# Transposes from the matrix engine to DMA, Q projection spread over the attention tiles, W_down in half blocks

## The chip, the cores and the metric

The kernel runs on one core of a Trainium2 chip. The metric is device time in microseconds (us). A run is one timed execution; medians over several runs are quoted, and verdicts use runs of the normal (fast) state. PE is the matrix engine (TensorE), DVE is VectorE, ACT is ScalarE, POOL is GpSimd, SP is SyncE, which issues the DMAs here.

## The reference

One transformer block with linear attention, S = 2048 tokens, D = 1024, 32 heads of 32, F = 3584, all in bf16:

```python
def _A_ref(x, wqkv, wo):                    # attention
    q, k, v = split_heads(x @ wqkv)         # shortened
    phi = lambda t: jnp.where(t > 0, t + 1, jnp.exp(t)) + 1e-6
    pq, pk = phi(q), phi(k)
    kv = jnp.einsum("bhsd,bhse->bhde", pk, v)
    z = jnp.einsum("bhsd->bhd", pk)
    num = jnp.einsum("bhqd,bhde->bhqe", pq, kv)
    den = jnp.einsum("bhqd,bhd->bhq", pq, z)[..., None] + 1e-6
    return merge_heads(num / den) @ wo      # shortened

h  = x + _A_ref(_layernorm(x), A_wqkv, A_wo)
n  = _layernorm(h)
gate = n @ W_gate; gate = gate * (gate > 0)
h2 = h + (gate * (n @ W_up)) @ W_down
```

(The last three lines are condensed from the reference's second function.)

## The kernel before

It has five stages: a start in which weights and the first rows of x arrive; K and V projections for 16 tiles of 128 tokens, accumulating `kv`; the Q projection of four blocks of 512 tokens together with attention (`nd` computes numerator and denominator and divides, `wo_h` projects and adds x); gate and up products in a Strassen-like form with seven products per block; and the down product in the same form. The matrix products here contract over the partitions (the first axis of a tile), so three tensors must be turned: normalised x (`xn` to `xnT`), the attention output (`o_sb` to `oT`) and normalised h (`hn`). Before, PE turns all of them in 128x128 blocks, 384 in all, and ScalarE (in the first tile VectorE too) copies the result out of PSUM, the memory that PE writes to.

```python
            xn = awork.tile([P, D], BF16, tag="xn", name="xn")
            nc.vector.tensor_scalar(out=xn[:], in0=x_sb[:], scalar1=mv[:, 0:1], scalar2=rstd[:],
                                    op0=ALU.subtract, op1=ALU.mult)
            pt = ps_tp()
            for kc in range(KC):
                nc.tensor.transpose(pt[:, kc, :], xn[:, kc * P:(kc + 1) * P], ident[:])
                if t == 0 and KC >= 2 and kc == KC // 2 - 1:
                    nc.vector.tensor_copy(out=xnT[:, 0:KC // 2, t * P:(t + 1) * P], in_=pt[:, 0:KC // 2, :])
            if t == 0 and KC >= 2:
                nc.scalar.copy(out=xnT[:, KC // 2:KC, t * P:(t + 1) * P], in_=pt[:, KC // 2:KC, :])
            else:
                nc.scalar.copy(out=xnT[:, :, t * P:(t + 1) * P], in_=pt[:])
    # ... cut ...
        ln_T(0)
        for g in range(NTB):
            pks = {}
            for tt in range(TPB):
                t = g * TPB + tt
                if t + 1 < ST:
                    ln_T(t + 1)
                pks[t] = kproj(t)
            for tt in range(TPB):
                t = g * TPB + tt
                vproj_kv(t, pks.pop(t))
            if g < NQA - 1:
                q_proj(g, ps_mm)
        for c in range(KC):
            bnk, i = divmod(c, GPB)
            nc.vector.tensor_tensor(out=kvz[:, c, :], in0=kv_ps[bnk][:, i * NDW:(i + 1) * NDW],
                                    in1=mask[:], op=ALU.mult)
        q_proj(NQA - 1, ps_mm)

    q_proj_rest = range(NQA, NTB)
    for b in q_proj_rest:
        q_proj(b, ps_y)
    qctx.close()
    # ... cut ...
        def nd():
            # ...
            for cs in nd_groups:
                ng = len(cs)
                ps = ps_x("nd")
                for k, c in enumerate(cs):
                    nc.tensor.matmul(ps[:, k * NDW:(k + 1) * NDW], lhsT=pqT[:, c, t * P:(t + 1) * P],
                                     rhs=kvz[:, c, :], start=True, stop=True)
                ndv = ps[:, 0:ng * NDW].rearrange("p (g w) -> p g w", w=NDW)
                den_sb = bsmall.tile([P, GPB, HPC], FP32, tag="den_sb", name="den_sb")
                nc.vector.tensor_scalar_add(out=den_sb[:, :ng, :], in0=ndv[:, :, P:NDW], scalar1=DEN_EPS)
                rd = bsmall.tile([P, GPB, HPC], FP32, tag="rd", name="rd")
                nc.vector.reciprocal(out=rd[:, :ng, :], in_=den_sb[:, :ng, :])
                nc.vector.tensor_tensor(
                    out=o_sb[:, cs[0] * P:(cs[-1] + 1) * P].rearrange("p (g h e) -> p g h e", g=ng, h=HPC),
                    in0=ndv[:, :, 0:P].rearrange("p g (h e) -> p g h e", h=HPC),
                    in1=rd[:, :ng, :].unsqueeze(3).to_broadcast([P, ng, HPC, Dh]),
                    op=ALU.mult)
    # ... cut ...
        def oT():
            pt = ps_tp()
            for c in range(KC):
                nc.tensor.transpose(pt[:, c, :], st["o"][:, c * P:(c + 1) * P], ident[:])
            st["oT"] = bwork.tile([P, KC, P], BF16, tag="oT", name="oT")
            nc.scalar.copy(out=st["oT"][:], in_=pt[:])

        def wo_h():
            x_sb = bwork.tile([P, D], BF16, tag="x_res", name="x_res")
            nc.sync.dma_start(out=x_sb[:], in_=xf[t * P:(t + 1) * P, :])
            h_sb = bwork.tile([P, D], BF16, tag="h", name="h")
            nwo = D // NW
            stats = bsmall.tile([P, nwo, nc.vector.BN_STATS_DIM], FP32, tag="stats2", name="stats2")
            for j in range(nwo):
                ps = ps_y("attn")
                for c in range(KC):
                    nc.tensor.matmul(ps[:, :NW], lhsT=st["oT"][:, c, :], rhs=wo_sb[:, c, j * NW:(j + 1) * NW],
                                     start=(c == 0), stop=(c == KC - 1))
    # ... cut ...
        def hnT():
            pt2 = ps_tp()
            for kc in range(KC):
                nc.tensor.transpose(pt2[:, kc, :], st["hn"][:, kc * P:(kc + 1) * P], ident[:])
            for j in range(2):
                nc.scalar.copy(out=hnq[s][i][j][:, :, r:r + P], in_=pt2[:, j * KH:(j + 1) * KH, :])
    # ... cut ...
    LAG = (0, 1, 1, 3)
    for step in range(ST + max(LAG)):
        for k in range(4):
            n = step - LAG[k]
            if 0 <= n < ST:
                stages[n][k]()
                if k == 3 and (n + 1) % (ST // NS) == 0:
                    hn_sums(n // (ST // NS))
    # ... cut ...
        def snap(ps, nm):
            m = mwork.tile([P, 2, SW], FP32, tag=nm, name=nm)
            nc.scalar.copy(out=m[:], in_=ps[:])
            return m
    # ... cut ...
        for k, h in ((0, 0), (1, 0), (0, 1), (1, 1)):
            x = dpool.tile([P, FH, DW], BF16, tag="wd", bufs=5, name="wd")
            nc.sync.dma_start(out=x[:], in_=wd_v[:, k * FH:(k + 1) * FH, h * DW:(h + 1) * DW])
            b.append(x)
        b11, b21, b12, b22 = b
```

The lag table runs the four stages of attention tiles in a software pipeline: in a step, tile n's `nd` is followed by `oT` and `wo_h` of tile n−1 and `hnT` of tile n−3. `_xy`, `ps_x`, `ps_y` and `ps_tp` give out PSUM banks.

Of the kernel before, what the change touches and what calls it, by code (L numbers as in the profile page):

```python
# [8 lines left out]
ALU = mybir.AluOpType  # L9
# [22 lines left out]
def block_kernel(ctx: ExitStack, tc: tile.TileContext, x, wqkv, wo, wg, wu, wd, out, H: int):  # L32
# [7 lines left out]
    assert Dh == 32 and D % P == 0 and S % P == 0 and F % P == 0  # L40
# [4 lines left out]
    TB = min(512, S)  # L45
    NTB = S // TB
    TPB = TB // P
    HB = min(256, TB)
    NHB = TB // HB
    NW = min(512, D)  # L50
    NKB = D // NW
    CPB = NW // P
    NDW = P + HPC
    GPB = 512 // NDW
    n_kv_banks = (KC + GPB - 1) // GPB
    assert TPB * H <= 512

# [9 lines left out]
    for hh in range(HPC):  # L67
        nc.gpsimd.memset(mask[hh * Dh:(hh + 1) * Dh, hh * Dh:(hh + 1) * Dh], 1.0)
        nc.gpsimd.memset(mask[hh * Dh:(hh + 1) * Dh, P + hh:P + hh + 1], 1.0)

    psctx = ExitStack()
    pspool = psctx.enter_context(tc.tile_pool(name="ps", bufs=1, space=PSUM))
    _xy = [0]

    def ps_tp():
        return pspool.tile([P, KC, P], BF16, tag="tp", bufs=2, name="tp")

    def ps_x(nm="x"):
        return pspool.tile([P, 512], FP32, tag="x", bufs=2, name=nm)

    def ps_y(nm="y"):
        return pspool.tile([P, 512], FP32, tag="y", bufs=4, name=nm)

    def ps_xy(nm="xy"):
        _xy[0] += 1
        return ps_x(nm) if _xy[0] % 3 != 0 else ps_y(nm)
# [5 lines left out]
    wo_sb = pq_pool.tile([P, KC, D], BF16, name="wo_sb")  # L92

    def phi_from_psum(ps_ap, dst_ap, pool, width):
        e = pool.tile([P, width], FP32, tag="phi_e", name="phi_e")
        nc.scalar.activation(out=e[:], in_=ps_ap, func=ACT.Exp)  # L96
        e2 = pool.tile([P, width], FP32, tag="phi_e2", name="phi_e2")
# [5 lines left out]
    qctx = ExitStack()  # L103
    qpool = qctx.enter_context(tc.tile_pool(name="qpool", bufs=1))
    qwork = qctx.enter_context(tc.tile_pool(name="qwork", bufs=2))
    wq_sb = qpool.tile([P, KC, D], BF16, name="wq_sb")
    xnT = qpool.tile([P, KC, S], BF16, name="xnT")
    wqkv_v = wqkv.rearrange("(kc p) n -> p kc n", p=P)

    def q_proj(b, ps_fn):  # L110
        for c in range(KC):
            ps = ps_fn("qp")
            for kc in range(KC):
                nc.tensor.matmul(ps[:, :TB], lhsT=wq_sb[:, kc, c * P:(c + 1) * P],  # L114
                                 rhs=xnT[:, kc, b * TB:(b + 1) * TB],
                                 start=(kc == 0), stop=(kc == KC - 1))
            phi_from_psum(ps[:, :TB], pqT[:, c, b * TB:(b + 1) * TB], qwork, TB)

    NQA = min(2, NTB)

    with ExitStack() as actx:
        apool = actx.enter_context(tc.tile_pool(name="apool", bufs=1))
        xpool = actx.enter_context(tc.tile_pool(name="xpool", bufs=min(6, ST)))
        awork = actx.enter_context(tc.tile_pool(name="awork", bufs=2))
        asmall = actx.enter_context(tc.tile_pool(name="asmall", bufs=4))

        ps_mm = ps_xy
        wkv_sb = apool.tile([P, KC, 2 * D], BF16, name="wkv_sb")
        kv_ps = [ps_y("kv_ps") for _ in range(n_kv_banks)]

# [6 lines left out]

        load_x(0)
        nxt = 1
        for j in range(NKB):  # L140
            nc.sync.dma_start(out=wkv_sb[:, :, j * NW:(j + 1) * NW],
                              in_=wqkv_v[:, :, D + j * NW:D + (j + 1) * NW])
            if nxt < min(TPB, ST):
                load_x(nxt)
                nxt += 1
        while nxt < min(TPB, ST):
            load_x(nxt)
            nxt += 1
        for j in range(NKB, 2 * NKB):
            nc.sync.dma_start(out=wkv_sb[:, :, j * NW:(j + 1) * NW],  # L150
                              in_=wqkv_v[:, :, D + j * NW:D + (j + 1) * NW])
        while nxt < min(6, ST):
            load_x(nxt)
            nxt += 1
        for j in range(NKB):
            nc.sync.dma_start(out=wq_sb[:, :, j * NW:(j + 1) * NW], in_=wqkv_v[:, :, j * NW:(j + 1) * NW])
        nc.sync.dma_start(out=wo_sb[:], in_=wo.rearrange("(kc p) n -> p kc n", p=P))

        def ln_T(t):
# [3 lines left out]
            nsub = (D + 511) // 512  # L163
            fm = D // nsub
            stats = asmall.tile([P, nsub, nc.vector.BN_STATS_DIM], FP32, tag="stats", name="stats")
            for i in range(nsub):
                nc.vector.bn_stats(out=stats[:, i, :], in_=x_sb[:, i * fm:(i + 1) * fm])  # L167
            mv = asmall.tile([P, nc.vector.BN_AGGR_DIM], FP32, tag="mv", name="mv")
            nc.vector.bn_aggr(out=mv[:], in_=stats[:])
            lnv = asmall.tile([P, 1], FP32, tag="lnv", name="lnv")  # L170
            nc.scalar.activation(out=lnv[:], in_=mv[:, 1:2], func=ACT.Ln, bias=LN_EPS, scale=1.0)
            rstd = asmall.tile([P, 1], FP32, tag="rstd", name="rstd")
            nc.scalar.activation(out=rstd[:], in_=lnv[:], func=ACT.Exp, scale=-0.5)
            xn = awork.tile([P, D], BF16, tag="xn", name="xn")
            nc.vector.tensor_scalar(out=xn[:], in0=x_sb[:], scalar1=mv[:, 0:1], scalar2=rstd[:],  # L175
                                    op0=ALU.subtract, op1=ALU.mult)
            pt = ps_tp()
            for kc in range(KC):
                nc.tensor.transpose(pt[:, kc, :], xn[:, kc * P:(kc + 1) * P], ident[:])  # L179
# [442 lines left out]
```

## Time and profile before

| | before |
|---|---|
| median of the first three runs | 828.26 us (827.77 to 830.4) |
| profiled run, span | 825.0 us |
| PE busy | 782.2 us (95%) |
| largest single PE wait | 8.0 us, for the first block of W_down |

The page's head and its line for the engines: busy time, share of the span, and number of instructions of each engine.

```profile
span 825.0 us, 10025 instructions
...
PE 782.2 (95%) x4016; PEld 369.1 (45%) x4016; DVE 506.7 (61%) x845; ACT 216.2 (26%) x337; POOL 3.6 (0%) x31
```

PE works 95% of the time, so there are 43 us of gaps to win, and beyond them only work taken off PE. The next view lists what PE waited for: the waiting group, the releaser, total us, how many waits, the longest.

```profile
engine line waited for: us in total, times, longest us
PE attn L315 <- ACT oT L304: 10.7, 15, 1.1
PE accA L510 <- DMA wd<-in_B_W_down_dram: 8.0, 1, 8.0
PE tp L179 <- DVE xn L175: 6.3, 2, 6.1
PE nd L286 <- DVE o_sb L293: 4.8, 5, 1.3
PE tp L335 <- DVE hn L328: 2.4, 1, 2.4
```

In attention PE waits for ScalarE's copies of the turned attention output (10.7 us in 15 waits) and for the division on VectorE (4.8). At the first down product it waits 8.0 us once, for a DMA of W_down.

Where PE is not the limit shows in windows cut at the stages: start, K/V, the two Q blocks after it, attention, gate/up, down. Each line gives the window, its length, each engine's busy us with the number of instructions, the granted PE clock (1.00 is full), the mean busy share of the DMA engines, and GB/s.

```profile
core 0: us, PE busy (x) PEld busy (x) DVE busy (x) ACT busy (x) POOL busy (x), PEclk, DMA share, GB/s
0.00:10.60 10.60, 1.98 (x16) 1.55 (x17) 4.37 (x9) 2.68 (x6) 1.58 (x17) 1.00 0.89 294
10.60:153.80 143.20, 143.00 (x820) 70.67 (x818) 68.85 (x139) 61.48 (x115) 2.00 (x14) 1.00 0.20 67
153.80:196.50 42.70, 41.38 (x194) 18.68 (x193) 30.96 (x68) 13.73 (x23) 0.00 (x0) 1.00 0.44 118
196.50:298.60 102.10, 82.88 (x641) 47.18 (x640) 91.17 (x248) 36.59 (x81) 0.00 (x0) 0.98 0.22 76
298.60:649.50 350.90, 341.72 (x1569) 154.07 (x1569) 218.50 (x300) 101.72 (x112) 0.00 (x0) 0.99 0.19 58
649.50:825.00 175.50, 171.25 (x784) 76.93 (x784) 92.79 (x85) 0.00 (x0) 0.00 (x0) 0.99 0.49 162
```

In K/V PE is busy 143.0 of 143.2 us: there, work removed from PE is time removed. In attention (196.5 to 298.6) PE is busy 82.88 of 102.1 us and VectorE 91.17. Just before it, in the Q blocks, PE is full (41.38 of 42.7) and VectorE is not.

The groups of PE's transposes (line, engine, operation, names, shapes, count, then busy us, mean ns, idle time before):

```profile
line engine op names shapes xcount | busy us, mean ns | idle before us <-releasers
...
L179 PE MATMUL tp<-ident,xn 128*128 128x128 bf16 x128 | 11.1, 230 | 8.6 <-DVE xn L175 6.3 <-DVE xnT L181 2.3
L302 PE MATMUL tp<-ident,o_sb 128*128 128x128 bf16 x128 | 10.7, 218 | 0.0
L335 PE MATMUL tp<-ident,hn 128*128 128x128 bf16 x128 | 9.9, 219 | 2.4 <-DVE hn L328 2.4
```

They cost 31.7 us of PE, or 83 ns each (11.1 / 128 = 87, 9.9 / 128 = 77); the mean of one record, about 220 ns, includes pipelined overlap and must not be multiplied by the count. Last, two DMA issues, for scale (size, and median us from issue to landing):

```profile
DMA packets 75678, 74.04 MB, mean 90 GB/s; under 512 B 3440, under 2 KB 67952, under 8 KB 75120
...
x_res<-in_A_x_dram SPq DMA_DIRECT2D x16, 256.0 KB, 2.8
...
h_dram_1891<-h SPq DMA_DIRECT2D x1, 256.0 KB, 2.0
```

### The profile page before, as it was taken

The page shows a single profiled execution, that of the slowest core. Times are in us where ns is not written, and L with a number is a line of the kernel's source. Part 1 is how long each engine was busy: PE and PEld are TensorE (multiplying, and loading weights), DVE is VectorE, ACT ScalarE, POOL GpSimd, SP SyncE. Part 2 cuts the span into 40 slices and gives each one's busy share as a digit, 9 for nine tenths or more (in the row PEclk, how much of TensorE's full clock was granted, in tenths as well). Part 3 has the DMA queues.
Part 4 walks back from the last instruction along what each step waited for, and adds up shares of the span by engine and source line. Part 5 has one row for each costly group of instructions (what it writes and reads, how often), then busy time and mean ns, then how long its engine had stood idle before and what let it go on. Part 6 is the DMA issues. An engine that isn't in the chain of part 4 may idle for free.

```text
span 825.0 us, 10025 instructions
## 1 busy us (share of the span) xinstructions
PE 782.2 (95%) x4016; PEld 369.1 (45%) x4016; DVE 506.7 (61%) x845; ACT 216.2 (26%) x337; POOL 3.6 (0%) x31
## 2 busy tenths in 40 slices
PE   5999999998897979999999999999999699999998
PEld 3445554443454534444444444444444244444443
DVE  5756314386999965567657556765754784329832
ACT  3435434332334333322323332333332000000000
POOL 0000000000000000000000000000000000000000
PEclk9999999999999989999999999999999899999999
DMA  9700000530222200040401304040000983892001
GB/s 323 250 14 26 1 1 1 152 92 0 97 83 79 89 25 14 20 127 27 122 26 56 84 20 128 25 122 27 20 19 20 300 267 120 273 340 97 26 33 45
DMA packets 75678, 74.04 MB, mean 90 GB/s; under 512 B 3440, under 2 KB 67952, under 8 KB 75120
## 3 DMA queue, kind: packets, MB, share of 16 engines
q1 hardware_dynamic: 75632, 73.41, 27.9%
q8 instruction: 31, 0.51, 0.3%
q14 instruction: 15, 0.12, 0.1%
HBM read 57.67 MB, written 15.73 MB: 89 GB/s over the span
## 4 chain that ended last, share of the span: by engine, by line
PE 59%; DVE 2%; DMA 2%; issue 1%; ACT 0%; SPq 0%; ACTq 0%
PE A L396 24%; PE E L396 12%; PE accA L510 10%; PE Dp L396 6%; PE accE L510 6%; PE accD L510 1%; DMA wd<-in_B_W_down_dram 1%; DMA hres<-h_dram_1898 1%; DVE s_6330 L534 0%; DVE hh L536 0%; DVE o L522 0%; DVE wd L548 0%; DVE s_6331 L535 0%; ACT u_5732 L410 0%; DVE hh_5749 L447 0%
## 5 line engine op out<-in xcount | busy, mean ns | idle before, releaser
L510 PEld LDWEIGHTS <-hh 128*128 128x128 bf16 (+1 forms) x560 | 55.1, 99 | 75.5 <-issue 10.6
L510 PE MATMUL accA<-wd,hh 128*128 128x512 f16 (+1 forms) x336 | 74.9, 385 | 8.0 <-DMA wd<-in_B_W_down_dram 8.0
L315 PE MATMUL attn<-wo_sb,oT 128*128 128x512 bf16 x256 | 61.2, 387 | 10.8 <-ACT oT L304 10.7
L396 PEld LDWEIGHTS <-tg 128*128 128x128 f16 x448 | 43.8, 98 | 54.2 <-issue 1.4
L396 PEld LDWEIGHTS <-tu 128*128 128x128 f16 x448 | 43.8, 98 | 52.9
L205 PE MATMUL vp<-wkv_sb,xnT 128*128 128x512 bf16 x256 | 59.8, 379 | 0.0
L192 PE MATMUL kp<-wkv_sb,xnT 128*128 128x512 bf16 x256 | 59.6, 388 | 0.0
L114 PE MATMUL qp<-xnT,wq_sb 128*128 128x512 bf16 x256 | 56.2, 379 | 1.3 <-DVE pqT L100 1.3
L396 PEld LDWEIGHTS <-wg 128*128 128x128 bf16 x336 | 33.2, 99 | 41.6 <-issue 2.9
L396 PEld LDWEIGHTS <-wu 128*128 128x128 bf16 x336 | 33.2, 99 | 40.9 <-issue 2.2
L315 PEld LDWEIGHTS <-oT 128*128 128x128 bf16 x256 | 23.6, 99 | 38.2 <-ACT oT L304 13.6
L114 PEld LDWEIGHTS <-wq_sb 128*128 128x128 bf16 x256 | 24.9, 98 | 30.9 <-issue 1.9
L192 PEld LDWEIGHTS <-xnT 128*128 128x128 bf16 x256 | 25.0, 100 | 28.0 <-issue 2.2
L205 PEld LDWEIGHTS <-xnT 128*128 128x128 bf16 x256 | 24.0, 97 | 24.6
L445 ACT ACTIVATE rg<-A 128x512 bf16<-128x512 f32 x28 | 16.7, 597 | 68.1 <-PE A L396 68.1
L304 ACT COPY oT<-tp 128x1024 bf16<-128x1024 bf16 x16 | 16.2, 1012 | 55.9 <-PE tp L302 55.9
L417 DVE SCALAR_TENSOR_TENSOR hh<-gu 128x512 bf16<-128x512 bf16 x42 | 29.0, 690 | 1.0
L96 ACT ACTIVATE phi_e<-qp 128x512 f32<-128x512 f32 x32 | 19.1, 597 | 39.1 <-PE qp L114 37.8
L175 DVE TENSOR_SCALAR xn<-x_sb,mv,rstd 128x1024 bf16<-128x1024 bf16 x16 | 8.7, 544 | 33.4 <-PE tp L179 31.1
L208 ACT CAST v_sb<-vp 128x512 bf16<-128x512 f32 x32 | 18.7, 585 | 39.8 <-PE vp L205 39.6
L167 DVE BATCH_NORM_STATS2 stats<-x_sb 128x6 f32<-128x512 bf16 x32 | 20.4, 671 | 9.8 <-DMA x_sb<-in_A_x_dram 9.8
L96 ACT ACTIVATE phi_e<-kp 128x512 f32<-128x512 f32 x32 | 19.1, 596 | 27.0 <-PE kp L192 27.0
(589 smaller groups left out, 1250.4 us busy)
## 6 DMA issues: line engine op xcount, KB each, us to landing
wd<-in_B_W_down_dram SPq DMA_DIRECT2D x8, 1792.0 KB, 9.7
wg<-in_B_W_gate_dram SPq DMA_DIRECT2D x14, 512.0 KB, 5.0
wu<-in_B_W_up_dram SPq DMA_DIRECT2D x14, 512.0 KB, 6.7
x_sb<-in_A_x_dram SPq DMA_DIRECT2D x16, 256.0 KB, 7.8
wkv_sb<-in_A_wqkv_dram SPq DMA_DIRECT2D x4, 1024.0 KB, 8.9
x_res<-in_A_x_dram SPq DMA_DIRECT2D x16, 256.0 KB, 2.8
out_dram<-o SPq DMA_DIRECT2D x32, 128.0 KB, 1.8
wq_sb<-in_A_wqkv_dram SPq DMA_DIRECT2D x2, 1024.0 KB, 11.0
```

The costliest lines, as they stand in the source:

```text
L96: nc.scalar.activation(out=e[:], in_=ps_ap, func=ACT.Exp)
L114: nc.tensor.matmul(ps[:, :TB], lhsT=wq_sb[:, kc, c * P:(c + 1) * P], rhs=xnT[:, kc, b * TB:(b + 1) * TB], start=(kc == 0), stop=(kc == KC ...
L167: nc.vector.bn_stats(out=stats[:, i, :], in_=x_sb[:, i * fm:(i + 1) * fm])
L192: nc.tensor.matmul(ps[:, :NW], lhsT=xnT[:, kc, t * P:(t + 1) * P], rhs=wkv_sb[:, kc, j * NW:(j + 1) * NW], start=(kc == 0), stop=(kc == KC ...
L205: nc.tensor.matmul(ps[:, :NW], lhsT=xnT[:, kc, t * P:(t + 1) * P], rhs=wkv_sb[:, kc, j * NW:(j + 1) * NW], start=(kc == 0), stop=(kc == KC ...
L208: nc.scalar.copy(out=v_sb[:, jj * CPB:(jj + 1) * CPB, 0:P], in_=ps[:, :NW].rearrange("p (c e) -> p c e", e=P))
L304: nc.scalar.copy(out=st["oT"][:], in_=pt[:])
L315: nc.tensor.matmul(ps[:, :NW], lhsT=st["oT"][:, c, :], rhs=wo_sb[:, c, j * NW:(j + 1) * NW], start=(c == 0), stop=(c == KC - 1))
L396: nc.tensor.matmul(ps[:, x, :], lhsT=w[x][m - 1][:, kc, :], rhs=left[m - 1][:, kc, :], start=(start and kc == 0), stop=(kc == KH - 1), ski ...
L417: nc.vector.scalar_tensor_tensor(out=d, in0=gu[:, 0, :], scalar=0.0, in1=gu[:, 1, :], op0=ALU.max, op1=ALU.mult)
L445: nc.scalar.activation(out=rg[:], in_=A[:, 0, :], func=ACT.Relu)
L510: nc.tensor.matmul(acc[:], lhsT=lhs[:, f, tt * P:(tt + 1) * P], rhs=rhs[:, f, :], start=(start and f == 0), stop=(f == FH - 1), skip_group ...
```

## The change

The intent is to take three things off PE's path:

1. Transposes: only x's first four tiles stay on PE (32 transposes); the other 12 tiles of `xn` and all 16 tiles of `o_sb` and of `hn` go by a transposing DMA of 256 KB each, 44 in all, all issued by SP.
2. Q projection: one block runs ahead, the other three are cut into 24 column groups and put between attention steps, two per step in the first twelve steps. `nd` uses one four-bank PSUM tile, one reciprocal per tile in place of three, and ScalarE adds the epsilon. The lag of `wo_h` grows from 1 to 2.
3. W_down: loaded in half blocks; the first half block is prefetched during the last gate/up group, and the down product runs over half blocks.

The core of the diff:

```diff
-            pt = ps_tp()
-            for kc in range(KC):
-                nc.tensor.transpose(pt[:, kc, :], xn[:, kc * P:(kc + 1) * P], ident[:])
-                if t == 0 and KC >= 2 and kc == KC // 2 - 1:
-                    nc.vector.tensor_copy(out=xnT[:, 0:KC // 2, t * P:(t + 1) * P], in_=pt[:, 0:KC // 2, :])
-            if t == 0 and KC >= 2:
-                nc.scalar.copy(out=xnT[:, KC // 2:KC, t * P:(t + 1) * P], in_=pt[:, KC // 2:KC, :])
-            else:
-                nc.scalar.copy(out=xnT[:, :, t * P:(t + 1) * P], in_=pt[:])
+            layernorm(x_sb, stats, xn, asmall)
+            if t >= PE_T:
+                nc.sync.dma_start_transpose(out=xnT[:, :, t * P:(t + 1) * P], in_=xn[:])
+                return
+            for i in range(2):
+                pt = bank("tp", BF16, [P, KH, P])
+                for kc in range(KH):
+                    nc.tensor.transpose(pt[:, kc, :], xn[:, (i * KH + kc) * P:(i * KH + kc + 1) * P], ident[:])
+                (nc.scalar.copy if i else nc.vector.tensor_copy)(
+                    out=xnT[:, i * KH:(i + 1) * KH, t * P:(t + 1) * P], in_=pt[:])
# ... cut ...
-        ln_T(0)
-        for g in range(NTB):
+        PE_T = 4
+        AHEAD = 2
+        for t in range(AHEAD):
+            ln_T(t)
+        for g in range(ST // NT):
             pks = {}
-            for tt in range(TPB):
-                t = g * TPB + tt
-                if t + 1 < ST:
-                    ln_T(t + 1)
+            for t in range(g * NT, (g + 1) * NT):
+                if t + AHEAD < ST:
+                    ln_T(t + AHEAD)
                 pks[t] = kproj(t)
-            for tt in range(TPB):
-                t = g * TPB + tt
+            for t in range(g * NT, (g + 1) * NT):
                 vproj_kv(t, pks.pop(t))
-            if g < NQA - 1:
-                q_proj(g, ps_mm)
# ... cut ...
-        q_proj(NQA - 1, ps_mm)
-
-    q_proj_rest = range(NQA, NTB)
-    for b in q_proj_rest:
-        q_proj(b, ps_y)
-    qctx.close()
# ... cut ...
+        for c in range(KC):
+            q_proj(qblocks[0], c)
# ... cut ...
-            for cs in nd_groups:
-                ng = len(cs)
-                ps = ps_x("nd")
-                for k, c in enumerate(cs):
-                    nc.tensor.matmul(ps[:, k * NDW:(k + 1) * NDW], lhsT=pqT[:, c, t * P:(t + 1) * P],
-                                     rhs=kvz[:, c, :], start=True, stop=True)
-                ndv = ps[:, 0:ng * NDW].rearrange("p (g w) -> p g w", w=NDW)
-                den_sb = bsmall.tile([P, GPB, HPC], FP32, tag="den_sb", name="den_sb")
-                nc.vector.tensor_scalar_add(out=den_sb[:, :ng, :], in0=ndv[:, :, P:NDW], scalar1=DEN_EPS)
-                rd = bsmall.tile([P, GPB, HPC], FP32, tag="rd", name="rd")
-                nc.vector.reciprocal(out=rd[:, :ng, :], in_=den_sb[:, :ng, :])
+            ps = ndpool.tile([P, NB, NW], FP32, tag="nd", name="nd")
+            for c in range(KC):
+                bnk, k = divmod(c, CPB)
+                nc.tensor.matmul(ps[:, bnk, k * NDW:(k + 1) * NDW], lhsT=pqT[:, c, t * P:(t + 1) * P],
+                                 rhs=kvz[:, c, :], start=True, stop=True)
+            ndv = ps[:, :, 0:CPB * NDW].rearrange("p b (k w) -> p b k w", w=NDW)
+            den = bsmall.tile([P, NB, CPB, HPC], FP32, tag="den", name="den")
+            nc.scalar.activation(out=den[:], in_=ndv[:, :, :, P:NDW], func=ACT.Identity, bias=deps[:], scale=1.0)
+            rd = bsmall.tile([P, NB, CPB, HPC], FP32, tag="rd", name="rd")
+            nc.vector.reciprocal(out=rd[:], in_=den[:])
# ... cut ...
         def oT():
-            pt = ps_tp()
-            for c in range(KC):
-                nc.tensor.transpose(pt[:, c, :], st["o"][:, c * P:(c + 1) * P], ident[:])
             st["oT"] = bwork.tile([P, KC, P], BF16, tag="oT", name="oT")
-            nc.scalar.copy(out=st["oT"][:], in_=pt[:])
-
-        def wo_h():
+            nc.sync.dma_start_transpose(out=st["oT"][:], in_=st["o"][:])
             x_sb = bwork.tile([P, D], BF16, tag="x_res", name="x_res")
             nc.sync.dma_start(out=x_sb[:], in_=xf[t * P:(t + 1) * P, :])
+            st["x"] = x_sb
+
# ... cut ...
-        def hnT():
-            pt2 = ps_tp()
-            for kc in range(KC):
-                nc.tensor.transpose(pt2[:, kc, :], st["hn"][:, kc * P:(kc + 1) * P], ident[:])
-            for j in range(2):
-                nc.scalar.copy(out=hnq[s][i][j][:, :, r:r + P], in_=pt2[:, j * KH:(j + 1) * KH, :])
# ... cut ...
+        def hn_T():
+            nc.sync.dma_start_transpose(out=hnT[s][i][:, :, r:r + P], in_=st["hn"][:])
# ... cut ...
-    LAG = (0, 1, 1, 3)
+    LAG = (0, 1, 2, 3)
# ... cut ...
+        qb, qc = divmod(step * 2, KC)
+        if qb + 1 < len(qblocks):
+            q_proj(qblocks[qb + 1], qc)
+            q_proj(qblocks[qb + 1], qc + 1)
+            if qb + 2 == len(qblocks) and qc + 2 == KC:
+                qctx.close()
# ... cut ...
+    prepool = ctx.enter_context(tc.tile_pool(name="prepool", bufs=1, side="right"))
# ... cut ...
+    def load_wd(k, h, x, pool=None):
+
+        w = (pool or dpool).tile([P, FD, DW], BF16, tag="wd", bufs=None if pool else 9, name="wd")
+        f0 = k * FH + x * FD
+        nc.sync.dma_start(out=w[:], in_=wd_v[:, f0:f0 + FD, h * DW:(h + 1) * DW])
+        return w
# ... cut ...
-        def snap(ps, nm):
-            m = mwork.tile([P, 2, SW], FP32, tag=nm, name=nm)
+        def snap(ps):
+            m = mwork.tile([P, 2, SW], FP32, tag="snap", bufs=4, name="snap")
             nc.scalar.copy(out=m[:], in_=ps[:])
             return m
```

The rest of the diff renames, moves pools to other sides of memory, splits PSUM differently, and reorders the down product's loads and sums to half blocks.

## The prediction

> What bounds it now. The page shows PE busy 782.2 of 825.0 us (95%), and PE holds 59% of the chain that ended last, so time falls only by taking work or gaps off PE. Its gaps sum to 43 us. They lie, by stretches, at the start (8.6 us idle in the first 25), in attention (195 to 300 us), around 635 to 660 us (9.2), and at the end (3.4). In attention PE is busy about 82 of 105 us, VectorE about 95: VectorE-bound. PE waits there for oT copies (10.7 us), o_sb (4.8), hn (2.4). At 649 us PE waits 8.0 us for W_down, and the granted clock falls to 0.86 in that stretch.
>
> What changes.
> (1) PE transposes: 384 become 32. By group they cost 11.1 + 10.7 + 9.9 = 31.7 us of PE, 83 ns each; removing 352 saves 29 us.
> (2) 44 DMA transposes of 256 KB, all from one queue. A plain 256 KB store took 2.0 us, a load 2.8 us to landing; I estimate 3 us (2 to 5) for a transpose. The Trainium skill, "Advanced Engine Details and Errata", section X-Bar Transpose (TRN2), calls them as fast as regular DMAs; "VectorE: DVE Perf Modes", The three transpose paths, gives 1309 ns for one 128x128 block. A tile has eight; if those ran one after another, it would be 10 us.
> (3) Q blocks (192 matmuls, 41 us of PE; 24 phi pairs at 0.43 + 0.69 = 27 us of VectorE) move into attention. The denominator add goes to ScalarE (7.0 us off VectorE) and 48 reciprocals become 16 (10.0 to about 3.4). Attention with Q then needs about 109 us of PE and 115 to 120 of VectorE; before it took about 41 + 105. Saving 20 to 32 us, transposes included.
> (4) First K/V stage: 96 transposes off PE, 8 us. Against it, PE's order now has three tiles' transposes ahead of the first K matmul, so the start waits for x tile 2 behind 2 MB of weights: 2 to 3 us lost.
> (5) W_down: half the first block is there, and seven matmuls per token tile (6 us) cover the other half. The 8.0 us wait falls to 0 to 2, and most of the 2 to 3 us of slow clock behind it goes.
>
> Sum: 8 - 3 + 26 + 10 = 41 us off 828, so 787 us; range 768 to 814. Chances: faster 0.82, same 0.08, slower 0.10.
>
> What would show it. PE transposes 32, busy about 753 us. DMA transposes landing in 2 to 5 us. In attention VectorE near 90% and PE's longest waits now o_sb/oT behind it, above all in the last four tiles, where no Q work fills in and only 4 to 5 us lie between nd and wo. No W_down wait above 2 us. First K matmul near 14 us instead of 10.7.
>
> What would make it wrong. A transpose occupying the queue for more than about 3.5 us: each attention step (7.7 us of PE) needs two, issued in order with the x and h transfers, so at 5 us attention is DMA-bound, at 10 us the kernel is slower by over 100 us. In the K stage the xn buffers (two) tie VectorE, in order, to the transposes; slow ones would hold back phi and stall PE. Gate/up weight loads ahead of transposes could add a few us in the tail.

## The result, and the profile after

| | before | after |
|---|---|---|
| median, us (same rounds) | 828.74 (827.77 to 830.4, 4 runs) | 793.39 (789.91 to 794.96, 4 runs) |
| ratio | 1 | 0.9566, 95% interval 0.9529 to 0.9602 |
| span of the profiled run | 825.0 | 792.9 |

A ratio here is the mean time of one kernel's fast runs over the mean time of the other's of the same rounds, so not quite the ratio of the medians. The change is 4.3% faster; the prediction was 787 us, 768 to 814. The profiled run of after is its slowest (794.96 us) and that of before is a fast one (827.12 us), so stage differences below add up to 32.1 us, not to the 35.3 us between the medians. The four runs of after differ by 5 us, and the mean clock granted to PE differs with them: 789.91 us at 0.998, 794.96 us at 0.991. The stretches of half clock that the trace below shows are those of its slowest run.

The engines after:

```profile
span 792.9 us, 9229 instructions
...
PE 756.3 (95%) x3601; PEld 349.4 (44%) x3664; DVE 493.7 (62%) x752; ACT 176.4 (22%) x293; POOL 3.9 (0%) x32
```

PE has 25.9 us less to do and is still 95% busy: the time that its work gave up was given up by the span too. (A few matmul records are missing from a trace, so counts are not exact.) PE's longest waits after:

```profile
PE tp L176 <- DVE xn L119: 12.0, 3, 6.1
PE attn L287 <- DMA oT<-o_sb: 8.3, 3, 4.0
PE A L372 <- ACT snap L386: 4.5, 3, 2.3
```

The W_down wait is gone. The wait for ScalarE's copies became a wait for the transposing DMA, 8.3 us in only three waits. New are 4.5 us for `snap`, a copy by ScalarE in gate/up. The start (`xn`) costs more than before. The stages after: start, K/V, Q with attention while there is Q work, the tail of attention without it, gate/up, down.

```profile
0.00:14.90 14.90, 2.92 (x25) 2.40 (x26) 8.12 (x18) 3.97 (x11) 1.62 (x18) 1.00 0.94 307
14.90:139.30 124.40, 122.49 (x639) 58.67 (x651) 57.17 (x118) 42.20 (x90) 2.24 (x14) 1.00 0.37 97
139.30:236.00 96.70, 95.60 (x511) 46.05 (x519) 84.81 (x164) 24.22 (x62) 0.00 (x0) 1.00 0.47 104
236.00:271.30 35.30, 25.90 (x122) 11.63 (x121) 27.09 (x58) 3.98 (x17) 0.00 (x0) 0.90 1.04 243
271.30:619.10 347.80, 340.31 (x1540) 154.02 (x1570) 217.20 (x310) 102.04 (x114) 0.00 (x0) 0.99 0.21 59
619.10:792.90 173.80, 169.06 (x775) 76.60 (x784) 99.32 (x89) 0.00 (x0) 0.00 (x0) 1.00 0.51 171
```

While Q work lasts (139.3 to 236.0), PE is busy 95.6 of 96.7 us. In the tail after it (236.0 to 271.3) PE is busy only 25.9 of 35.3 us, the DMA engines are full (a share of 1.04) and the granted clock is 0.90.

To compare stages I count the Q block that before runs inside its K/V window (64 matmuls, estimated at 13.7 us: the Q window after it has PE busy 41.38 us with 193 weight loads, one for each matmul) with attention. "Alone" columns are experiments described below: e3 has neither interleaving nor DMA transposes, e1 only interleaving, e2 only DMA transposes; all three have the rest of the change.

| us of the profiled run | start | K/V | Q + attention | gate/up | down | sum |
|---|---|---|---|---|---|---|
| before | 10.6 | 129.5 | 158.5 | 350.9 (8.0 of it the W_down wait) | 175.5 | 825.0 |
| e3: neither | 14.8 | 131.0 | 145.0 | 342.9 | 173.5 | 807.2 |
| e1: interleaving alone | 14.9 | 130.8 | 139.4 | 344.0 | 173.5 | 802.6 |
| e2: DMA transposes alone | 14.9 | 124.1 | 146.6 | 342.4 | 173.6 | 801.6 |
| after: both | 14.9 | 124.4 | 132.0 | 347.8 | 173.8 | 792.9 |

From before to after: start −4.3, K/V +5.1, Q and attention +26.5, gate/up +3.1, down +1.7 us saved.

The DMA view after has the transposes' landing times (packets by size first):

```profile
DMA packets 122266, 85.53 MB, mean 108 GB/s; under 512 B 50032, under 2 KB 114544, under 8 KB 121712
...
oT<-o_sb SPq DMA_TRANSPOSE x16, 3.1
h_dram_78<-h SPq DMA_DIRECT2D x1, 256.0 KB, 2.1
...
xnT<-xn SPq DMA_TRANSPOSE x12, 3.8
```

A transpose lands 3.1 us (`oT`) to 3.8 us (`xnT`) after its issue at the median. The plain 256 KB store shown took 2.1 us; all sixteen stores of `h` took 2.0 to 6.6, half of them over 2.5. It makes many small packets: those under 512 B rose from 3,440 to 50,032.

The tail of attention on SP's queue and on PE (start, us, engine, line, operation, names; in brackets the idle time before and its releaser):

```profile
240.39 0.52 SPq L343 DMA_DIRECT2D wg<-in_B_W_gate_dram  x1
...
242.38 1.60 SPq L276 DMA_TRANSPOSE oT<-o_sb  x1
```

```profile
247.62 1.72 PE L287 MATMUL attn<-wo_sb,oT 128*128 128x512 bf16 x4 [4.01 <-DMA oT<-o_sb]
```

The transpose of one of the last tiles is issued at 242.38, after a load of gate weights, and PE waits 4.01 us for `oT` until 247.62: the tail has no Q work to fill the time.

The first `snap` of gate/up, on ScalarE, and PE behind it:

```profile
279.67 1.01 ACT L386 COPY snap<-A 128x1024 f32<-128x1024 f32 x1 [6.54 <-DMA hn_1497<-hn]
```

```profile
280.74 1.02 PE L372 MATMUL A<-hs_1499,tg 128*128 128x512 f16 x4 [2.31 <-ACT snap L386]
281.60 1.54 PE L372 MATMUL A<-hs_1499,tu 128*128 128x512 f16 x4
284.24 1.86 PE L372 MATMUL A<-hs_1500,tg 128*128 128x512 f16 x4 [1.10 <-ACT snap L386]
285.90 1.91 PE L372 MATMUL A<-hs_1500,tu 128*128 128x512 f16 x4
```

ScalarE waits 6.54 us, not for its input but for a transposing DMA of `hn`. PE waits 2.31 us behind it. What follows starts at full speed and then falls to half: from 280.74 to 281.60, four matmuls start in 0.86 us (0.215 each); from 284.24 to 287.60, eight take 3.36 us (0.42 each). The granted clock is 0.50 from 282 to 284 us and 0.52 from 284 to 289. (Before has such a stretch at the start of gate/up too: 0.66 from 296 to 306 us.) The Trainium skill, "TensorE: Matmul & The Clock Gate", Part 1, gives 426.7 ns cold and 215.7 ns warm for this size; the trace agrees with both.

### The profile page after: what moved, and what is told of

The parts are those of the page before. It is cut to its first block, busy times and chain, and to the rows that moved or that the text cites. A ratio compares the mean times of both kernels' runs of the same rounds, so it can differ in the third digit from the quotient of the medians.

```text
span 792.9 us, 9229 instructions
## 1 busy us (share of the span) xinstructions
PE 756.3 (95%) x3601; PEld 349.4 (44%) x3664; DVE 493.7 (62%) x752; ACT 176.4 (22%) x293; POOL 3.9 (0%) x32
## 4 chain that ended last, share of the span: by engine, by line
PE 60%; DVE 2%; issue 2%; DMA 1%; ACT 0%; ACTq 0%; DVEq 0%
PE A L372 24%; PE E L372 12%; PE accA L469 11%; PE Dp L372 6%; PE accE L469 6%; PE accD L469 2%; DMA hn_1497<-hn 1%; DVE s_5784 L522 0%; ACT snap L386 0%; DVE o L483 0%; DVE hh L523 0%; DVE s_5783 L521 0%; DVE t_5786 L532 0%; DVE wd L531 0%; DVE gu L391 0%
## 5 line engine op out<-in xcount | busy, mean ns | idle before, releaser
L391 DVE TENSOR_TENSOR gu<-E,snap 128x1024 bf16<-128x1024 f32 x56 | 68.5, 1224 | 105.7 <-ACT snap L386 99.3
L386 ACT COPY snap<-A 128x1024 f32<-128x1024 f32 x84 | 84.9, 1012 | 174.3 <-PE A L372 150.6
L469 PE MATMUL accA<-wd,hh 128*128 128x512 f16 (+1 forms) x333 | 73.2, 379 | 1.6 <-DVE gu L391 1.4
L185 PE MATMUL kp<-wkv_sb,xnT 128*128 128x512 bf16 x249 | 58.0, 389 | 0.3
L391 DVE TENSOR_TENSOR gu<-Dp,snap 128x1024 bf16<-128x1024 f32 x28 | 34.3, 1224 | 14.1 <-PE Dp L372 14.1
L289 DVE TENSOR_TENSOR h<-attn,x_res 128x512 bf16<-128x512 f32 x32 | 21.6, 679 | 6.0 <-PE attn L287 6.0
```

The source lines that it names most:

```text
L185: nc.tensor.matmul(ps[:], lhsT=xnT[:, kc, t * P:(t + 1) * P], rhs=wkv_sb[:, kc, j * NW:(j + 1) * NW], start=(kc == 0), stop=(kc == KC - 1))
L289: nc.vector.tensor_tensor(out=h_sb[:, j * NW:(j + 1) * NW], in0=ps[:], in1=st["x"][:, j * NW:(j + 1) * NW], op=ALU.add)
L391: nc.vector.tensor_tensor(out=gu[:], in0=ps[:], in1=m[:], op=ALU.add)
L469: nc.tensor.matmul(accs[tt][:], lhsT=lhs[:, half * FD + f, tt * P:(tt + 1) * P], rhs=rhs[half][:, f, :], start=(start and half == 0 and f ...
```

## The experiments

My theory before the experiments was this. (a) The parts pay by stage: DMA transposes pay in K/V, where PE is full; interleaving pays in attention; the two need each other there, for with Q mixed in PE is the limit again. (b) The 6 us missing against my prediction lie at the start, in the tail (transposes queue behind weight loads) and at the start of gate/up (`snap`). The rivals were that one part does all of it, that VectorE is the limit in attention and the new division the reason, and that the losses are due to the DMA transposes' own speed. Each experiment starts from the kernel after; "the kernel before" ran in each batch too (827.33, 828.02 and 828.81 us in e1 to e4, e5 to e8, e9 to e12). All twelve gave correct results. The kernel after ran in none of these batches, so it is compared by its ratio.

### e1: transposes back on PE, Q still interleaved

```diff
-                nc.sync.dma_start_transpose(out=xnT[:, :, t * P:(t + 1) * P], in_=xn[:])
+                pt = bank("tp", BF16, [P, KC, P])
+                for kc in range(KC):
+                    nc.tensor.transpose(pt[:, kc, :], xn[:, kc * P:(kc + 1) * P], ident[:])
+                nc.scalar.copy(out=xnT[:, :, t * P:(t + 1) * P], in_=pt[:])
# likewise for oT and hnT
```

> The changed kernel with all 48 tile transposes on PE again; Q blocks stay interleaved and W_down stays in halves. Theory (the transposes are the gain, because attention with Q interleaved is limited by PE): 352 transposes at 83 ns put 29 us back on PE, 8 us in the K/V stage and 21 us in attention; the waits for oT and for the first snap after a DMA transpose (8.3 + 4.5 us in the trace of the change) go away. So 805 to 815 us. Rival (the interleaving is the gain; VectorE limits attention and PE's transposes fit in its gaps): at most 8 us more than the change, 793 to 801 us.

Measured: 804.82 us, ratio 0.9732 (0.9711 to 0.9753): just outside the low edge of what my theory expected, and outside the rival's range; the DMA transposes are worth about 1.7% on top of interleaving. K/V is 6.4 us longer than after, Q with attention 7.4. The stretch with Q work:

```profile
160.00:250.40 90.40, 89.50 (x588) 48.00 (x598) 78.10 (x144) 39.61 (x73) 0.00 (x0) 1.00 0.16 53
```

PE is busy 89.50 of 90.40 us. With Q interleaved PE is the limit, so transposes on PE lengthen the stage. Their cost is below their 83 ns each: while Q work lasts, 160 of them are 12.3 us of PE records, and the stage is 8.0 us longer than in after (104.7 against 96.7).

### e2: Q first, transposes by DMA

```diff
-        for c in range(KC):
-            q_proj(qblocks[0], c)
+        for qb in qblocks:
+            for c in range(KC):
+                q_proj(qb, c)
# and the q_proj calls between attention steps removed
```

> The changed kernel with all four Q blocks ahead of attention; the transposes stay on the DMA. Theory (both parts matter, because without Q matmuls PE idles behind VectorE in attention): attention takes VectorE about 98 us and the three Q blocks 41 us before it, against 132 us for both together now, so 7 to 12 us more, 800 to 806 us. Rival (interleaving is nearly the whole gain): 812 us or more. Rival (interleaving is worth nothing, the transposes are all): within 3 us of the change.

Measured: 804.33 us, ratio 0.9723 (0.9702 to 0.9743), as expected: interleaving is worth 1.6% on top of DMA transposes. The attention stage:

```profile
193.90:285.60 91.70, 70.38 (x377) 33.57 (x383) 77.33 (x153) 11.18 (x47) 0.00 (x0) 0.91 0.90 212
```

PE is busy 70.38 of 91.70 us and VectorE 77.33; PE waits 11.2 us for `oT` and 8.4 for `o_sb`. The DMA share is 0.90.

### e3: both undone

The edits of e1 and e2 together.

> Both undone: transposes on PE and Q blocks first; only W_down in halves, the den on ScalarE and the new start remain. If the three parts are all of the change: before minus the W_down wait (8 us) and some 3 us of VectorE work in attention, plus 4 us for the later start, 818 to 825 us. If the two parts add up, it is e1 plus e2 less the change; if they cover for each other, it is more than that sum.

Measured: 809.91 us, ratio 0.979 (0.9769 to 0.981). This is a miss: I expected 818 to 825. The kernel with neither main part is 17.4 us faster than before. Its attention stage:

```profile
200.70:290.80 90.10, 79.32 (x631) 47.61 (x641) 82.64 (x168) 41.13 (x81) 0.00 (x0) 0.98 0.44 132
```

With e1, e2 and e3 the two parts can be put in a square. Over e3, DMA transposes alone give 0.67% of before's time (0.979 − 0.9723), interleaving alone 0.58%, both together 2.24% (0.979 − 0.9566). They help each other, by about 1%, 8 us. The stages show where: in K/V the transposes give 6.4 to 6.9 us with or without interleaving. In Q with attention, interleaving alone saves 5.6 us (145.0 to 139.4), DMA transposes alone nothing (145.0 to 146.6), both 13.0 (to 132.0). With Q first, PE is not the limit of attention. What the DMA takes off it comes back as waits: 11.2 us for `oT` and 8.4 for `o_sb` in e2, where e3 has none for `oT` and 6.1 for `o_sb`, and the granted clock is 0.91 against 0.98.

The 17.4 us of e3 were unexpected. By the traces they are: the W_down wait (8.0 us) gone; the 10.7 us of waits for `oT` copies gone (they do not appear in e3 or e11); against it, a start 4.2 us later. That adds up to 14.5 us. By the table of stages e3's profiled run is 17.8 us shorter than before's: of the 3.3 us left, 2.0 lie in the down product and 2.8 in Q with attention, and K/V is 1.5 longer. The 2.8 may be the new division (e11 is slower than e3 by 0.2% of before's time, 1.8 us, with overlapping intervals). The `oT` waits went because `wo_h` comes one step later after its transpose (lag 2 in place of 1), I think; no run sets only the lag back, so that is argued and not shown.

### e4: W_down not prefetched

```diff
-        if g == FH // GP - 1:
-            first_wd = load_wd(0, 0, 0, prepool)
# the first half block is loaded where the down product begins, with one buffer more in the common pool
```

> The changed kernel without the prefetch of the first half block of W_down (it is loaded where the down stage begins, as the other half blocks). Theory: PE waits again for W_down, but for a half block, 5 us and not 8, and the clock falls after it: 4 to 7 us more, 797 to 801 us. Rival (halving alone did it): within 2 us of the change.

Measured: 797.33 us, ratio 0.9645 (0.9617 to 0.9673), as expected. PE waits 5.4 us once for a half block. So half blocks alone cut the wait from 8.0 to 5.4, and the prefetch takes the rest.

This run happens to show something about the clock as well. Its edit leaves the start of gate/up alone, and PE waits for `snap` there just as in after, 4.5 us in three waits:

```profile
278.93 1.02 PE L371 MATMUL A<-hs,tg 128*128 128x512 f16 x4 [2.33 <-ACT snap L385]
281.92 1.02 PE L371 MATMUL A<-hs,tg 128*128 128x512 f16 x4 [1.10 <-ACT snap L385]
```

The granted clock is 1.00 throughout (278 to 292 us), and gate/up without the W_down wait takes 343.6 us, not 347.8. So the waits for `snap` do not by themselves bring the half clock, and about 4 us of after's gate/up come with it.

### e5: the start, with two tiles of transposes ahead of the first K product in place of three

```diff
         AHEAD = 2
-        for t in range(AHEAD):
-            ln_T(t)
+        ln_T(0)
+        done = 1
@@
-                if t + AHEAD < ST:
-                    ln_T(t + AHEAD)
+                while done < ST and done <= t + (1 if t < 2 else AHEAD):
+                    ln_T(done)
+                    done += 1
```

> The changed kernel with one edit: the layernorm and transposes of tile 2 are written after the K projection of tile 0, as before, so PE's order has two tiles' transposes ahead of the first K matmul and not three. Theory (the later start is a fixed loss of the whole kernel): the first K matmul goes from 14.9 to about 10.7 us and the end comes 3 to 4 us earlier, 789 to 791 us. Rival (the loss is made up later, because the next tiles wait for x anyway): first matmul earlier, but a new wait for xn of 3 us or more behind it and a total within 1 us of the change.

Measured: 788.32 us, ratio 0.9525 (0.9507 to 0.9542), a little better than expected. The interval overlaps that of after by a hair, so the timing alone leaves some doubt; the traces do not: the first K matmul starts at 10.8 us in place of 14.9, and the first gate/up matmul at 267.2 in place of 271.3, 4.1 us earlier in both places. The start's loss is PE's instruction order: the transposes of one more tile, the third, stood ahead of the first product, and that tile's x was still behind weights in the queue. (The profiled runs differ by 7.1 us: gate/up is 3.8 us shorter here, 344.0 us, with no half clock in it, which the edit does not touch.)

### e6: gate/up weights kept back until the last tile's layernorm

```diff
+            if t == order[-1]:
+                nc.gpsimd.tensor_copy(out=gate[:], in_=st["hn"][:, 0:1])
@@
+                if g < 2:
+                    nc.gpsimd.tensor_copy(out=w_sb[:, 0, h, 0:1], in_=gate[:])
```

> The changed kernel, but the loads of the first two gate/up weight groups (4 MB) wait for the layernorm of the last attention tile, so no weights share the DMA with the last transposes. Theory (the waits for oT in the tail are contention with these loads): the waits of PE for oT fall from 8.3 us to 2 us or less, the last wo matmul ends 4 to 7 us earlier than 269.9 us; gate/up then starts late because its weights come late, so the total is about that of the change, 791 to 799 us. Rival (the 3 us latency of a transpose is itself too long for the tail's spacing): waits for oT stay at 6 us or more and the total goes to 800 us or above.

Measured: 792.0 us, ratio 0.957 (0.9552 to 0.9588), the same as after, as it had to be: the weights are now late themselves. What the run is for is the trace. PE's waits in it:

```profile
PE A L377 <- DMA wg<-in_B_W_gate_dram: 9.3, 1, 9.3
PE attn L288 <- DMA oT<-o_sb: 2.3, 1, 2.3
```

The waits for `oT` fall from 8.3 to 2.3 us, and the last `wo` matmul ends at 261.9 in place of 269.9. That is 8.0 us earlier, more than the 4 to 7 expected, and the wait is a little above the 2 us expected. So it is mostly the weight loads in front of them that delay the transposes in the tail, not the transposes' own speed. The price, 9.3 us waiting for `wg`, eats it.

### e7: the last four attention outputs turned on PE

```diff
-            nc.sync.dma_start_transpose(out=st["oT"][:], in_=st["o"][:])
+            if order.index(t) >= 12:
+                pt = bank("tp", BF16, [P, KC, P])
+                for c in range(KC):
+                    nc.tensor.transpose(pt[:, c, :], st["o"][:, c * P:(c + 1) * P], ident[:])
+                nc.scalar.copy(out=st["oT"][:], in_=pt[:])
+            else:
+                nc.sync.dma_start_transpose(out=st["oT"][:], in_=st["o"][:])
```

> The changed kernel with the transposes of o for the last four attention tiles on PE (32 matmuls of 83 ns, 2.7 us). Theory (in the tail PE waits for transposes in the DMA queue, 8.3 us, and has time to do them itself): 3 to 6 us less, 787 to 790 us. Rival (VectorE is the limit of the tail and only the name of the wait changes): within 1.5 us of the change, with PE waiting for o_sb or for ScalarE's copy instead.

Measured: 786.63 us, ratio 0.95 (0.948 to 0.9521), slightly better than expected and clear of after's interval. The wait for the transposing DMA is gone, `wo` ends at 263.6, and 32 transposes on PE cost less than the DMA wait, since PE is idle there anyway.

### e8: memory of its own for `snap`

The pool that `snap` uses is placed, in the kernel after, on memory that attention's working tiles used; the program's wait list for the first `snap` names the last transposing DMA that reads `hn` (a build of the kernel shows it; in e8 the list no longer has it). This version gives `snap` a pool clear of it, and pays with one buffer less for two attention tiles:

```diff
-            x_sb = bwork.tile([P, D], BF16, tag="x_res", name="x_res")
+            x_sb = bwork.tile([P, D], BF16, tag="x_res", bufs=2, name="x_res")
@@
-            st["hn"] = bwork.tile([P, D], BF16, tag="hn", name="hn")
+            st["hn"] = bwork.tile([P, D], BF16, tag="hn", bufs=2, name="hn")
@@
+    snpool = mctx.enter_context(tc.tile_pool(name="snpool", bufs=4))
@@
-            m = mwork.tile([P, 2, SW], FP32, tag="snap", bufs=4, name="snap")
+            m = snpool.tile([P, 2, SW], FP32, tag="snap", bufs=4, name="snap")
```

> The changed kernel with the snap buffers of gate/up in memory that the Q stage freed long before, in place of memory that overlaps the attention tiles (x_res and hn get two buffers in place of three to make room). Theory (the first snap waits for the last DMA transpose only because the allocator put its buffer on the tile which that transpose reads): the 4.5 us wait of PE for snap at the start of gate/up and the slow clock behind it go, 3 to 5 us less, 788 to 790 us. Rival (the start of gate/up waits for something else as well, as the sums of the last tiles): the wait moves to another releaser and the total stays within 1 us.

Measured: 786.66 us, ratio 0.9507 (0.9489 to 0.9526), better than expected, just clear of after's interval. PE's wait for `snap` falls from 4.5 to 1.1 us, and gate/up takes 342.4 us in place of 347.8. Attention also ends earlier (267.0 against 269.9), perhaps because two buffers instead of three change the order of loads. That is not shown: e4, with three, ends it at 268.0. This part of the gain is not about `snap`. ScalarE's first `snap` now runs before the last transpose of `hn` is even issued:

```profile
270.39 1.01 ACT L387 COPY snap<-A 128x1024 f32<-128x1024 f32 x1
```

```profile
270.88 1.68 SPq L297 DMA_TRANSPOSE hn<-hn  x1
```

The reuse of memory is thus shown to be what holds `snap` back. It is not shown to bring the half clock: e4 has the same waits without it. Its gate/up of 343.6 us lies 1.2 us above e8's, so by the traces the larger part of the 5.4 us is the half clock that after's profiled run had.

### e9: sixteen transposes more than needed

The transposes of `o_sb` and `hn` of the first eight tiles are each issued a second time, into a tile that is overwritten later.

```diff
+            if n < 8:
+                nc.sync.dma_start_transpose(out=hnT[1][0][:, :, n % 4 * P:(n % 4 + 1) * P], in_=st["o"][:])
# and the same for hn
```

> The changed kernel in which each of the first eight attention tiles issues both of its DMA transposes a second time, into a block of hn that is overwritten later (16 extra transposes; the result stays correct). If a transpose occupies the DMA for about 1.65 us (an estimate: in 170 to 225 us the DMA is busy 0.64 of each 7.7 us step, less 1.6 us for two plain 256 KB transfers, over two transposes), four of them and the two transfers take 8.2 us a step: the DMA share of that stretch rises to about 1.0 and the total grows by 1 to 8 us. If it occupies 3.5 us or more, as the prediction feared, the steps with four need 15 us and the total grows by 50 us or more. If it costs what a plain transfer costs (0.8 us), nothing changes.

Measured: 794.91 us, ratio 0.9589 (0.9567 to 0.9611): 0.2% more than after, no clear change. The share of DMA rose less than the first estimate said (to 0.86, not to about 1.0), and growth by 50 us is ruled out. The stretch with the added transposes, in e9 and then in after:

```profile
155.00:236.00 81.00, 79.45 (x424) 38.45 (x432) 74.22 (x141) 19.23 (x53) 0.00 (x0) 1.00 0.86 176
```

```profile
155.00:236.00 81.00, 79.95 (x431) 38.80 (x439) 74.64 (x142) 19.44 (x54) 0.00 (x0) 1.00 0.56 124
```

All sixteen are issued in this stretch. The DMA share rises by 0.30 over 81 us; divided by 16 transposes, one occupies the 16 DMA engines for 1.52 us on average. It moves 256 KB, so 172 GB/s at full use. A plain load is at 307 / 0.94 = 327 GB/s in the start of after, 0.80 us for as much: a transpose takes nearly twice the DMA time. Packets rise by 1,056 per transpose. Still PE is as busy as in after: in this stretch there is room for them.

### e10: e5, e7 and e8 together

The three edits above, in one kernel.

> The changed kernel with the three repairs together: tile 2's transposes after the first K matmuls, o of the last four tiles transposed on PE, snap buffers in memory freed early. Alone they gave 5, 7 and 7 us; the last two share part of the stretch from 240 to 285 us. If the waits are separate, 775 to 780 us; if the last two were the same wait, 781 to 783.

Measured: 784.69 us, ratio 0.9476 (0.9457 to 0.9496), the fastest kernel measured and clear of after's interval; but a miss, for I expected 775 to 780. The gains do not add: e5 gave 0.4%, e7 0.7, e8 0.6 over after, all three 0.9. The trace has a new wait. On SP and on VectorE:

```profile
257.40 0.43 SPq L285 DMA_DIRECT2D x_res<-in_A_x_dram  x1
```

```profile
262.50 0.69 DVE L296 TENSOR_TENSOR h<-attn,x_res 128x512 bf16<-128x512 f32 x1 [2.93 <-issue]
```

With two `x_res` buffers, the last load of x can be issued only at 257.40; it lands 5.0 us later behind weights and transposes. VectorE is idle 2.93 us before the `h` that needs it, and PE then waits 4.45 us at its first gate/up matmul, at 265.29. The small memory won for `snap` was taken from the buffers that this tail needs. A version with three `x_res` buffers was not run, so what it would give stays open.

### e11 and e12: the old division, without and with the main parts

The epsilon and the reciprocals go back to VectorE, three groups per tile as in before, on e3 (e11) and on the kernel after (e12):

```diff
-            nc.scalar.activation(out=den[:], in_=ndv[:, :, :, P:NDW], func=ACT.Identity, bias=deps[:], scale=1.0)
-            rd = bsmall.tile([P, NB, CPB, HPC], FP32, tag="rd", name="rd")
-            nc.vector.reciprocal(out=rd[:], in_=den[:])
# and one four-bank PSUM tile; in their place, for each of three groups of heads:
+                nc.vector.tensor_scalar_add(out=den[:, :ng, :], in0=ndv[:, :, P:NDW], scalar1=DEN_EPS)
+                rd = bsmall.tile([P, GPB, HPC], FP32, tag="rd", name="rd")
+                nc.vector.reciprocal(out=rd[:, :ng, :], in_=den[:, :ng, :])
```

> The kernel with transposes on PE and Q first (e3), and the division by den as before: three groups a tile, den + eps and 1/den on VectorE, in place of one add on ScalarE, one reciprocal and two products. Theory (what is left between before and e3, 17.4 us, is the W_down wait of 8 us and VectorE's 13.6 us of small operations, less 4 us of later start, because attention without Q is limited by VectorE): 10 to 14 us more than e3, 820 to 824 us. Rival (that difference comes from the order of the stages, the lag of one more step): within 4 us of e3.

> The same undoing of the division on the changed kernel itself. VectorE's work in attention with Q goes from about 115 to 128 us against 112 us of PE, so VectorE is the limit again: 6 to 14 us more, 799 to 807 us. If PE stays the limit because the small operations fit in VectorE's gaps: within 3 us.

Measured: e11 812.83 us, ratio 0.9812 (0.9789 to 0.9836), overlapping e3's; e12 793.95 us, ratio 0.9581 (0.9562 to 0.96), the same as after. My theory that the lighter division carries the 17 us of e3 and that VectorE limits attention falls. In e11 about 2 us may be the division's, and the intervals leave room for none. The stretch with Q work in e12:

```profile
139.30:235.20 95.90, 94.79 (x506) 46.03 (x515) 87.82 (x233) 21.31 (x49) 0.00 (x0) 1.00 0.48 105
```

VectorE has 87.82 us to do in place of 84.81, and the stretch is 0.8 us shorter, not longer: PE, with 94.79 of 95.90, sets its length. One more thing is to be had from e12. In the tail its longest `oT` wait is 5.6 us, its tail is 40.5 us long, and then its `snap` wait is 1.9 us and its gate/up 342.3; the kernel after has 35.3 and 347.8. Tail and gate/up together are 382.8 and 383.1. In this pair, what is lost early is not lost again late, so the tail and the start of gate/up should be judged together, and gains of e7 and e8 can overlap. It is no rule: in e4 the two are 33.4 and 343.6 us (without its W_down wait), together 377.0.

## Why the prediction was right, point by point

The prediction of 787 us was 6 us too low, and the range held. Step by step:

- (1) PE's work: predicted about 753 us busy with 32 transposes left. Measured 756.3, so right.
- (2) The transpose: I estimated 3 us to landing, 2 to 5. Measured 3.1 and 3.8, so right. The fear that one could occupy the queue for over 3.5 us did not come true: SP spends 1.23 us on an issue of `oT` at the median, and the DMA engines 1.52 us on average. But in the tail, behind weight loads, an issue of `hn` took up to 3.33 us. The Trainium skill's figure in "VectorE: DVE Perf Modes", The three transpose paths, 1309 ns for one 128x128 block, does not multiply by eight: a tile's eight blocks land in 3.1 us together.
- (3) Attention: "Saving 20 to 32 us" (26 in the sum); measured 26.5. The size was right, the reason was in part wrong. I wrote that VectorE would be near 90% and the limit. It was busy 84.8 of 96.7 us (88%), but PE 95.6, and e12 shows that PE limits. I also did not cost the lag of `wo_h`. The tail went as described: the longest waits are for `oT`, in the last tiles.
- (4) K/V and start: 8 us predicted, 5.1 measured (6.4 to 6.9 for the transposes between kernels of the same order). At the start "2 to 3 us lost" was 4.3; the first K matmul was foreseen near 14 us and came at 14.9.
- (5) W_down: "0 to 2" us of wait, and none is left. But I booked 10 us for it, and gate/up and down together gave only 4.8. The step that failed is that nothing else would change in gate/up. The `snap` buffers lie on memory that a transposing DMA still reads: besides the W_down wait, PE idles 7.5 us in gate/up in place of 1.2 (window less busy time), 4.5 of them for `snap`. The half clock is no part of this difference, for both profiled runs have such a stretch there; it is most of the 5.4 us between after and e8.

The sum predicted was 41 us; the profiled runs give 32.1, the medians 35.3. The terms that were mis-sized are the start (1 to 2 us), K/V (about 3) and gate/up (about 5).

## What to carry to other kernels

Moving work off an engine pays only where that engine sets the time: here DMA transposes gave nothing in attention until the Q projection was mixed in and made PE the limit again, and then both gave more than their sum. A transposing DMA needs work to hide behind and a queue without bulk loads in front; at the end of a stage, where PE idles anyway, keep the transpose on PE. When a reader of a tile becomes a DMA, check which later buffers take over its memory, for they now wait for that DMA.

## What the Trainium skill lacked or had wrong

- "Advanced Engine Details and Errata", X-Bar Transpose (TRN2), says that transposing DMAs are as fast as regular ones, and expects 350 to 400 GB/s. The runs show 1.52 us of all DMA engines for 256 KB, 172 GB/s, against 0.80 us and 327 GB/s for plain loads in the same kernel. "DMA: Bandwidth & Descriptors", Latency and other measured facts, has 261 GB/s for a layout with a non-contiguous middle dimension, still above what the runs show.
- No page that I read gives a transpose's packet count: 1,056 per 256 KB here (e9 against after).
- "VectorE: DVE Perf Modes", The three transpose paths, compares 390 ns on TensorE and 1309 ns by DMA for one block. In a stream the numbers are others: 83 ns of PE per block, and 3.1 us to landing for eight blocks by DMA, with 1.23 us on the issuing engine.
- "DMA: Bandwidth & Descriptors", Rules for kernel authors, says that a transpose next to ordinary DMAs needs nothing. It speaks of correctness, and there the runs agree. It lacks the cost in time: `oT` landed in 3.0 to 6.3 us in after, the longest in the tail with weight loads around it, and in at most 4.4 us in e6, where those were kept back.
- "TensorE: Matmul & The Clock Gate", Part 1, puts the slow clock after an idle window of about 3.4 us. Its speeds agree (0.42 and 0.215 us), but in the kernel after the slow stretch set in after a PE gap of 2.31 us, behind a tail with many gaps (25.9 of 35.3 us busy). In e4 gaps of 2.33 and 1.10 us in the same place, behind a similar tail (25.6 of 33.4 us busy), left the clock at 1.00. So the gap alone does not decide it, and what does stays open.
- No page has the wait that a buffer inherits from the earlier user of its memory: here 6.54 us on ScalarE and 4.5 us of PE's time in after, gone but for 1.1 us in e8.
